# Splitting the stationary side of three float32 matmul groups into two halves of 64 columns

## The chip, the core and the metric

The kernel runs on one core of one Trainium2 chip. The metric is device time in microseconds (us) of one execution, the median of several. TensorE (PE) does the matrix products: the stationary operand is loaded into its array by a weight load (PEld in the profile), then the rows of the moving operand stream through it (PE). ScalarE (ACT), VectorE (DVE) and GpSimd (POOL) do the element-wise work, SyncE (SP) issues the transfers.

## The reference, cut to what matters

```python
X = np.fft.rfft(x, axis=1)                      # x: (8, 3136, 256)
Yr = Xr @ w_r - Xi @ w_i + b_r                  # complex 256 x 256 mix
Yi = Xr @ w_i + Xi @ w_r + b_i
Yr = np.sign(Yr) * np.maximum(np.abs(Yr) - 0.01, 0)   # Yi likewise
x = np.fft.irfft(Yr + 1j * Yi, n=3136, axis=1)
h = x.transpose(0, 2, 1) @ U @ V                # U: (3136, 32), V: (32, 3136)
u = x + h.transpose(0, 2, 1)
out = u + np.maximum(u @ w_ch1, 0) @ w_ch2      # 256 -> 1024 -> 256
```

## The kernel before

The transform of 3136 points is done as 49 times 64. For each of the 8 batches there are these stages, named by the letter that is in the names of their PSUM tiles:

- A (`psa`): the transform over 49 points, 98 partitions at a time.
- B (`psb`, function `b_mm`, and `b_early` for the first three of batch 0): the transform over 64 points with its twiddle factors. One unit takes two frequencies `k` and two halves `h` of the 256 channels, so four products: the stationary side is a 128x128 piece of the tile `t` (of `t0t` in batch 0), the moving side 128 columns of `fb`. A frequency-0 unit has a stationary side of only 64 rows (64x128).
- the mix (`psq`, `pst`), the shrinking, and C (`psc`), the inverse over 64 points.
- D (`psd`, function `d_unit`): the inverse over 49 points. One unit has four products: the stationary side is 98x128 of the tile `zt`, the moving side 130 columns of `dt` (`du` in batch 0): 98 of the transform and 32 that carry U.
- U (`psu`, function `make_ud`): once, 32 small products that make those 32 columns, 98x98 stationary by 32 moving.
- then, in windows of 512 tokens: V (`psv`), the first layer (`psy`, `psx`, `psz`; seven products in place of eight, in the manner of Strassen) and the second layer (`pso`).

There are two kinds of products. Most operands are split into a high and a low part of type float32r, and each product is done as three matmuls of the parts (`mm3`, `l1`, `l2_chunks`). B, D, U and the A stage of the first two batches multiply plain float32 in one instruction of the program, which the hardware profile shows as two passes, each with a weight load and a matmul of its own. So B and D have 384 + 512 = 896 instructions of 128 stationary columns, which are 1792 passes, and U has 32, which are 64 passes; the 64-row units of B (16 more instructions) are apart from these.

The order of all instructions is not written by hand. Every operation is first recorded with a cost (`_Program.cost`); then `order` and `forward` arrange the operations of each engine by list scheduling from these costs, and `trace` issues them, so that nearly everything in the profile has one line, L509 (L512 in the changed kernel). Operations on one PSUM tile that were recorded in a row stay together as a unit. For the PE the planner knows float32 matmuls as `port` operations; after them it charges `SWITCH` us once, and `STICK` makes it prefer to stay with them:

```python
free[e] = t + sum(op.cost for op in units[k])
if e == "pe":
    free[e] += SWITCH * (whole and not u.port)
```

In the built program 928 float32 instructions of B, D and U with full width stand in 146 unbroken groups on the PE (95 of them of 4 instructions, 25 of 8, 13 of 12, 10 of 16). Beside them five short visits of the 64-row units of B run in a 64x128 part of the array, and a few float32r matmuls of C, of the mix and of `pst` with a 64-column stationary side in its left 128x64 part.

Of the kernel before, what the change touches and what calls it, by code (L numbers as in the profile page):

```python
# [26 lines left out]
NP = 98  # L27
NI = 32
D = 256
R = 32  # L30
# [113 lines left out]


PASSES, LEAD, FILL = 12, 16.0, 200.0
SWITCH, STICK = 0.083, 5.0


CHANGES = ()  # L150
# [6 lines left out]
class _Program:  # L157
# [27 lines left out]
    def cost(self, op, out, ins):  # L185
        n = out.ids.size // out.shape[0] if isinstance(out, _View) else 1
        sb = not any(v.buf.space == "psum" for v in ins)
        op.move, op.port, op.fill = 0.0, False, 0
        if op.name == "dma_start":

            some = out if isinstance(out, _View) else ins[0]
            op.move = some.ids.size / 64000
            op.cost = 0.35 if op.eng == "act" else 0.5
            op.lag = 2.2 + op.move
        elif op.eng == "pe":
            if op.name == "matmul" and op.kw["lhsT"].dtype == F32:
                op.cost = 2 * max(0.111, 0.00084 * n)
                op.port = True
            else:
                op.cost = max(0.1118, 0.000422 * n)  # L200
            op.lag = 0.25
        elif op.eng == "act":
            op.cost = 0.17 + 0.000836 * n + (0.035 if sb else 0) + (0.09 if "bias" in op.kw else 0)
            op.lag = 0.1
        elif op.eng == "dve":

            op.port = sb and op.name != "transpose"
            slow = op.name == "transpose" and not sb
            op.cost = 0.155 + (0.00053 if op.name == "tensor_scalar" else 0.00168 if slow else 0.00104) * n
            op.lag = 0.1  # L210
        elif op.eng == "pool":
            op.port = op.name == "tensor_tensor"
            op.cost = 0.16 + (0.00222 if op.port else 0.0007) * n
            op.lag = 0.15
# [298 lines left out]
def fft_mix_moe_kernel(  # L513
# [21 lines left out]
    act, dve, pool, pe, dma = [prog.engine(e) for e in ("act", "dve", "pool", "pe", "sp")]  # L535
# [6 lines left out]
    def psm(shape, name):  # L542

        turn_m[0] += 1
        return ps_m.tile(shape, F32, tag=f"psm{turn_m[0] % 3}", name=name)
# [8 lines left out]
    def acopy(o, i):  # L554
        return act.activation(o, i, AF.Copy)
# [164 lines left out]
    def pairs(b):  # L720
        p = [(1 + 2 * q, 2) for q in range(12)]
        if shared(b):
            p.append((0, 2))
        elif b == 0 or b % 2 == 1:
            p.append((0, 1))
        return p
# [12 lines left out]
    def load_t(b, q):  # L739
        k0, n = pairs(b)[q]  # L740
        if b == 0:
            if (b, "fb", q) not in s_state:
                load_fb(b, q)
            ts = [[t0[h][:, k0 + k] for h in range(2)] for k in range(n)]
            s_state[b, q] = (ts, s_state.pop((b, "fb", q)))
            return
        t = fp.tile([128, 2, D], F32, tag="t", name=f"t_{b}_{q}")
        g = gd[b % 2]
        nk = n if k0 else 1
        dma.dma_start(t[0:64, 0:nk, :], g[k0 : k0 + nk].rearrange("k n d -> n k d"))  # L750
        if n > nk:
            dma.dma_start(t[0:64, 1, :], gd[(b + 1) % 2][0])
        if k0:
            dma.dma_start(t[64:128, 0:n, :], g[24 + k0 : 24 + k0 + n].rearrange("k n d -> n k d"))
        if (b, "fb", q) not in s_state:
            load_fb(b, q)
        ts = [[t[:, k, 128 * h : 128 * h + 128] for h in range(2)] for k in range(n)]
        s_state[b, q] = (ts, s_state.pop((b, "fb", q)))

    def ybuf(b, q, tag):  # L760

        tg = tag if b else dict(rl="xsh", ys="xsl")[tag]
        return fp.tile([128, 2, D], F32, tag=tg, name=f"{tag}_{b}_{q}", bufs=1)

    def b_early(q):

        load_t(0, q)
        ts, fbt = s_state[0, q]
        ps = psm([128, 2, 2, 128], f"psb_0_{q}")
        for k in range(2):  # L770
            pe.matmul(ps[:, 0, k, :], lhsT=ts[k][0], rhs=fbt[:, k, :], start=True, stop=True)
        s_state[0, "ps", q] = ps

    def b_mm(b, q):
        k0, n = pairs(b)[q]
        ts, fbt = s_state.pop((b, q))
        kk = 128 if k0 else 64
        early = s_state.pop((b, "ps", q), None)
        if early is not None:
            ps = early  # L780
        elif b:
            ps = ps_f.tile([128, 2, 2, 128], F32, tag="psf", name=f"psb_{b}_{q}")
        else:
            ps = psm([128, 2, 2, 128], f"psb_{b}_{q}")
        for h in range(2) if early is None else (1,):
            for k in range(n):
                pe.matmul(
                    ps[:, h, k, :],
                    lhsT=ts[k][h][:kk],
                    rhs=fbt[:kk, k if k0 else 0, :],  # L790
                    start=True,
                    stop=True,
                )
        return ps


# [230 lines left out]
    def d_load(b, t, du):  # L1027
        z_load(b, 2 * t)
        z_load(b, 2 * t + 1)
        if du is None:  # L1030
            dt_ = mp.tile([NP, TI, NP + R], F32, tag="dt", name=f"dt_{b}_{t}", bufs=2)
            i = slice(TI * t, TI * t + TI)
            dma.dma_start(dt_, dud[:, i, :])
        else:
            dt_ = du[t]
        return dt_

    def d_unit(b, i, du):
        i *= 2
        t, k = divmod(i, TI)  # L1040
        ahead = 1 if b else 3
        if i == 0:
            for c in range(ahead):
                s_state[b, "d", c] = d_load(b, c, du)
            p_state[b] = qp.tile([128, 2, R], F32, tag="pa", name=f"pa_{b}", bufs=2)
        if k == 0 and t + ahead < NT:
            s_state[b, "d", t + ahead] = d_load(b, t + ahead, du)
        if i % NH == 0:
            xq[b, i // NH] = qp.tile([128, 2, NH, NP], F32, tag="xq", name=f"xq_{b}_{i}", bufs=3)
        zt, dt_ = s_state[b, "z", i // 2], s_state[b, "d", t]  # L1050
        if b or i // 2 % 2:
            ps = ps_f.tile([128, 512], F32, tag="psf", name=f"psd_{b}_{i}")
        else:
            ps = psm([128, 512], f"psd_{b}_{i}")
        psv = ps[:, 0 : 2 * (2 * NP + R)].rearrange("p (h c) -> p h c", h=2)
        for h in range(2):
            for n in range(2):
                pe.matmul(
                    psv[:, h, n * NP : n * NP + NP + R],
                    lhsT=zt[:, n, 128 * h : 128 * h + 128],  # L1060
                    rhs=dt_[:, k + n, :],
                    start=h == 0 and n == 0,
                    stop=h == 1 and n == 1,
                    skip_group_check=True,
                )
        for h in range(2):
            c = h * (2 * NP + R)
            both = ps[:, c : c + 2 * (NP + R)].rearrange("p (n c) -> p n c", n=2)
            acopy(xq[b, i // NH][:, h, i % NH : i % NH + 2, :], both[:, :, 0:NP])
        pa = p_state[b]  # L1070
        if i == 0:
            dve.tensor_copy(pa, psv[:, :, NP : NP + R])
        else:
            dve.tensor_tensor(out=pa, in0=pa, in1=psv[:, :, NP : NP + R], op=ALU.add)
# [114 lines left out]
    for a in range(4):  # L1189
        v = (b_r, b_i)[a % 2]  # L1190
# [28 lines left out]
    us = mp.tile([NP, NI, R], F32, tag="rl", name="us", bufs=3)  # L1219
# [17 lines left out]
    fdt = qp.tile([NP, NI, NP], F32, tag="xq", name="fdt", bufs=3)  # L1237
# [10 lines left out]
    def make_ud(c):  # L1248
        ps = psm([128, 512], f"psu_{c}")
        for k in range(8):  # L1250
            pe.matmul(
                ps[:NP, 32 * k : 32 * k + 32],
                lhsT=fdt[:, 8 * c + k, :],
                rhs=us[:, 8 * c + k, :],
                start=True,
                stop=True,
            )
        for t in range(2):
            o = ps[:NP, 128 * t : 128 * t + 128]
            u = du[2 * c + t].rearrange("p (g i) c -> p g (i c)", i=2)  # L1260
            acopy(u[:, :, NP : NP + 2 * R], o.rearrange("p (g r) -> p g r", r=2 * R))
# [122 lines left out]
    def wait_2():  # L1384

        for c in range(4):
            make_ud(c)
            a_mm(1, c)
        for u in range(4, NI // 2):
            a_mm(1, u)  # L1390
# [308 lines left out]
    for w, prev, next_w in zip(turn_w, [None] + turn_w, turn_w[1:] + [None]):  # L1699
        b, j = divmod(w, NW)  # L1700
        if j == 0 and b < NB:
            assert not side
            side = [(6.5, lambda b=b: rest_unit(b))]
            if b + 1 < NB:
                start, mid, end = (1, 58, 84) if b else (18, 71, 86)

                side += bmc_spread(b + 1, start, mid - 6)
                if b + 2 < NB:
                    if shared(b + 1):
                        lo, hi = (21, 56) if b == 0 else (1, 39)  # L1710
                    else:
                        lo, hi = 45, 94
# [6 lines left out]
        for g in range(2):  # L1719
            l1s = l1_chunks(w, g)  # L1720
            new = l2_chunks(w, g)
            for k in range(4):
                for c in range(2):
                    n = WS * j + 8 * g + 2 * k + c
# [115 lines left out]
```

## Time and profile before

| | |
|---|---|
| median of 3 runs | 1624.22 us (1622.07 to 1627.01) |
| profiled execution | 1623.88 us, span in the profile 1622.1 us |
| PE busy | 1594.0 us (98%), 11112 matmul passes |
| weight loads busy | 1475.7 us (91%) |
| DVE, ACT, POOL busy | 73%, 62%, 35% |

The span is the time from the first to the last instruction of the program; it is 1.8 us shorter than the execution's own time. A matmul's record reaches from its start to the modelled end of its results, so that a record is longer than the step to the next matmul: the step of a group is (its length minus one record) divided by (its count minus 1).

### The profile page before, as it was taken

What the parts mean: (1) busy time and instruction counts of PE and PEld (TensorE: products, weight loads), DVE (VectorE), ACT (ScalarE), POOL (GpSimd) and SP (SyncE); (2) the same over time, 40 slices, a digit from 0 to 9 for tenths busy, and PEclk for the clock granted to TensorE, in tenths of its full rate; (3) what the DMA queues carried; (4) which work ended last, traced back from release to release, by engine and by line L of the source; (5) the groups of instructions that cost most, each with busy time, mean ns of one, the idle gap of its engine ahead of it and who ended that gap; (6) DMA issues with size and microseconds to landing.
All of it is one profiled execution on the core that took longest, in us unless ns stands there. A gap on an engine that the chain in (4) does not pass through costs nothing. (4 is left out here: it accounts for less than half of the span.)

```text
span 1622.1 us, 31847 instructions
## 1 busy us (share of the span) xinstructions
PE 1594.0 (98%) x11112; PEld 1475.7 (91%) x11112; DVE 1186.9 (73%) x2097; ACT 1005.1 (62%) x2187; POOL 566.5 (35%) x502
## 2 busy tenths in 40 slices
PE   8999999999999999999999999999999999999998
PEld 6979999998899999999889998999898999999997
DVE  6888777587856688577875777767785677857775
ACT  4875775565666676556666676556666666655553
POOL 2322552233433553124443554223343333312221
PEclk9999999999999999999999999999999999999999
DMA  8874555334663565414674466623557244620222
GB/s 250 237 245 116 161 170 141 114 102 131 178 200 121 146 184 140 142 53 111 170 204 137 132 174 163 166 62 92 144 148 219 83 114 132 161 77 16 54 72 53
DMA packets 271452, 223.63 MB, mean 138 GB/s; under 512 B 136986, under 2 KB 220608, under 8 KB 271292
## 3 DMA queue, kind: packets, MB, share of 16 engines
q1 hardware_dynamic: 268654, 220.73, 48.1%
q8 instruction: 89, 1.46, 0.4%
q10 hardware_dynamic: 2638, 0.86, 0.2%
q14 instruction: 71, 0.58, 0.1%
HBM read 121.36 MB, written 77.20 MB: 122 GB/s over the span
## 5 line engine op out<-in xcount | busy, mean ns | idle before, releaser
L509 PE MATMUL pso<-rh,w2t 128*128 128x512 f32 x1568 | 407.5, 382 | 0.6 <-DVE xq L509 0.6
L509 PEld LDWEIGHTS pso<-rh,w2t 128*128 128x128 f32 x1568 | 274.6, 190 | 27.6 <-DVE xq L509 1.0
L509 PE MATMUL pso<-rl,w2t 128*128 128x512 f32 x784 | 233.5, 379 | 0.5 <-DVE rl L509 0.5
L509 POOL TENSOR_TENSOR yl<-ys,yh 128x512 fp32r<-128x512 f32 (+1 forms) x101 | 132.0, 1307 | 211.0 <-ACT yh L509 190.6
L509 POOL TENSOR_TENSOR xl<-xt,xh 98x512 fp32r<-98x512 f32 x96 | 129.3, 1347 | 196.9 <-ACT xh L509 192.8
L509 DVE SCALAR_TENSOR_TENSOR rl<-s,rh 128x512 fp32r<-128x512 f32 x196 | 162.2, 839 | 11.5 <-ACT rh L509 10.7
L509 PEld LDWEIGHTS pso<-rl,w2t 128*128 128x128 f32 x784 | 148.0, 189 | 22.0 <-DVE rl L509 1.1
L509 ACT ACTIVATE rh<-s 128x512 fp32r<-128x512 f32 x196 | 121.7, 629 | 47.9 <-DVE s L509 46.3
L509 POOL TENSOR_TENSOR tl<-ts,th 128x256 fp32r<-128x256 f32 x88 | 70.3, 799 | 164.0 <-issue 70.1
L509 DVE TENSOR_TENSOR tb<-psq,bias 128x512 f32<-128x512 f32 x88 | 60.8, 691 | 88.6 <-DMA ys<-tb 48.9
L509 PE MATMUL psy<-odh,w1t 128*128 128x256 f32 x784 | 122.0, 278 | 3.3 <-DVE s L509 2.8
L509 PE MATMUL psq<-wmt,xsh 128*128 128x256 f32 (+1 forms) x704 | 122.6, 275 | 0.0
L509 PEld LDWEIGHTS psy<-odh,w1t 128*128 128x128 f32 x784 | 110.5, 191 | 11.8 <-DVE s L509 4.5
L509 ACT ACTIVATE yh<-ys 128x512 fp32r<-128x512 f32 (+1 forms) x101 | 63.4, 627 | 85.1 <-DMA ys<-tb 80.3
L509 PEld LDWEIGHTS psq<-wmt,xsh 128*128 128x128 f32 (+1 forms) x704 | 110.9, 191 | 3.0
L509 POOL TENSOR_TENSOR oal<-tt,oah 128x512 fp32r<-128x512 f32 x48 | 65.4, 1363 | 135.6 <-ACT oah L509 130.2
L509 PE MATMUL psd<-dt,zt 98*128 98x130 f32 x896 | 109.4, 275 | 2.7 <-DMA zt<-zd 1.9
L509 DVE TENSOR_TENSOR v<-v,psy 128x512 f32<-128x512 f32 x98 | 67.0, 683 | 60.5 <-ACT v L509 58.4
L509 PEld LDWEIGHTS psd<-dt,zt 98*128 98x128 f32 x896 | 105.9, 191 | 5.4 <-issue 2.7
L509 ACT ACTIVATE xq<-psd 128x196 f32<-128x196 f32 x256 | 72.0, 332 | 59.7 <-PE psd L509 59.3
L509 POOL TENSOR_TENSOR odl<-tt,odh 128x512 fp32r<-128x512 f32 x48 | 64.0, 1334 | 109.8 <-ACT odh L509 98.2
L509 PE MATMUL psq<-wmt,xsl 128*128 128x256 f32 (+1 forms) x352 | 97.2, 276 | 1.0 <-DVE xsl L509 0.9
(215 smaller groups left out, 4146.9 us busy)
## 6 DMA issues: line engine op xcount, KB each, us to landing
zt<-zd SPq DMA_DIRECT2D x128, 196.0 KB
zd<-zs SPq DMA_DIRECT2D x192, 128.0 KB
out_dram<-os SPq DMA_DIRECT2D x190, 128.0 KB
ys<-tb SPq DMA_DIRECT2D x350, 64.0 KB
t<-gd SPq DMA_DIRECT2D x168, 128.0 KB
xt<-in_x_dram SPq DMA_DIRECT2D x100, 196.0 KB
gd<-gs SPq DMA_DIRECT2D x96, 196.0 KB
fb<-in_fb_dram SPq DMA_DIRECT2D x96, 128.0 KB
```

Of the source, the lines that this page charges most:

```text
L509: call(*[real(a) for a in op.args], **{k: real(a) for k, a in op.kw.items()})
```

## The change

Each B, D and U product is written as two matmuls over 64 stationary columns each (64 and 34 for U). The moving side is the same for both. The first writes PSUM partitions 0 to 63, the second 64 to 127, so the first is built for the left 128x64 part of the array (position 0, 0) and the second for the right part (position 0, 64). The 64-row units of B stay whole. The planner's cost of such a half is 0.065 us where the whole was 0.222, and SWITCH is 0.35 in place of 0.083.

```diff
-SWITCH, STICK = 0.083, 5.0
+SWITCH, STICK = 0.35, 5.0
...
             if op.name == "matmul" and op.kw["lhsT"].dtype == F32:
-                op.cost = 2 * max(0.111, 0.00084 * n)
+                if op.kw["lhsT"].shape[1] <= 64:
+                    op.cost = max(0.065, 0.00042 * n)
+                else:
+                    op.cost = 2 * max(0.111, 0.00084 * n)
...
+    def b_half(o, t, f, cut=True):
+        for c in range(2) if cut else ():
+            v = slice(64 * c, 64 * c + 64)
+            pe.matmul(o[v], lhsT=t[:, v], rhs=f, start=True, stop=True)
+        if not cut:
+            pe.matmul(o, lhsT=t, rhs=f, start=True, stop=True)
...
-            pe.matmul(ps[:, 0, k, :], lhsT=ts[k][0], rhs=fbt[:, k, :], start=True, stop=True)
+            b_half(ps[:, 0, k, :], ts[k][0], fbt[:, k, :])
...
+                b_half(ps[:, h, k, :], ts[k][h][:kk], fbt[:kk, k if k0 else 0, :], k0 > 0)
...
-                pe.matmul(
-                    psv[:, h, n * NP : n * NP + NP + R],
-                    lhsT=zt[:, n, 128 * h : 128 * h + 128],
...
+                for c in range(2):
+                    pe.matmul(
+                        psv[64 * c : 64 * c + 64, h, n * NP : n * NP + NP + R],
+                        lhsT=zt[:, n, 128 * h + 64 * c : 128 * h + 64 * c + 64],
...
+            for lo, hi in ((0, 64), (64, NP)):
+                pe.matmul(
+                    ps[lo:hi, 32 * k : 32 * k + 32],
+                    lhsT=fdt[:, 8 * c + k, lo:hi],
...
```

In the changed program 1856 halves stand in 159 groups (103 of 8 halves, 31 of 16, 19 of 24, the rest other sizes): as many groups as before and some more, and the part of the array that an instruction is built for changes 339 times along the PE's order where it changed 24 times. The counts of transfers (1607 by SP), of ACT operations (2186) and of DVE and POOL operations are the same.

The PE's order at one B unit, the fourth of batch 4, before (names are tile, then its numbers; 128x128 is partitions written by columns moved):

```order
L509 MATMUL pst_2_9600<-wm0h,th_2_9564 128x256
L509 MATMUL pst_2_9600<-wm0l,th_2_9564 128x256
L509 MATMUL pst_2_9600<-wm0h,tl_2_9585 128x256
L509 MATMUL psb_3_9611<-fb_3_9394,t_3_9382 128x128 x4
L509 MATMUL psy_1_9408<-odh_9256,w1t 128x256 x4
L509 MATMUL psy_1_9408<-odl_9264,w1t 128x256 x2
L509 MATMUL pso_0_9481<-rh_0_1_9343,w2t 128x512
```

The four products stand alone between the mix and the first layer. Now the same unit on the PE:

```order
L512 MATMUL pso_0_10018<-rh_0_1_9866,w2t 128x512
L512 MATMUL pso_1_10021<-rh_0_1_9866,w2t 128x512
L512 MATMUL pso_0_10018<-rl_0_1_9888,w2t 128x512
L512 MATMUL pso_1_10021<-rl_0_1_9888,w2t 128x512
L512 MATMUL psb_3_10121<-fb_3_9928,t_3_9883 64x128 x8
L512 MATMUL psy_1_9913<-odh_9759,w1t 128x256 x4
L512 MATMUL psy_1_9913<-odl_9771,w1t 128x256 x2
```

Four matmuls became eight halves, which stand after a piece of the second layer; they are still a group by themselves.

The first D units of batch 4 on the PE, before (the first number of `psd` is the row pair `i`):

```order
L509 MATMUL pso_0_10899<-rl_1_0_10983,w2t 128x512
L509 MATMUL pso_1_10901<-rl_1_0_10983,w2t 128x512
L509 MATMUL psd_0_11061<-dt_0_10590,zt_0_10996 128x130 x4
L509 MATMUL psd_2_11071<-dt_0_10590,zt_1_11002 128x130 x4
L509 MATMUL psd_4_11084<-dt_1_10599,zt_2_11011 128x130 x4
L509 MATMUL psd_6_11098<-dt_1_10599,zt_3_11019 128x130 x4
L509 MATMUL psy_1_10868<-odh_10786,w1t 128x256 x4
L509 MATMUL psy_1_10868<-odl_10815,w1t 128x256 x2
L509 MATMUL psa_6_11121<-xh_6_11004,fah 98x512
```

and in the changed program:

```order
L512 MATMUL pso_0_11454<-rl_0_1_11405,w2t 128x512
L512 MATMUL pso_1_11456<-rl_0_1_11405,w2t 128x512
L512 MATMUL psd_0_11566<-dt_0_10752,zt_0_11507 64x130 x8
L512 MATMUL psd_2_11576<-dt_0_10752,zt_1_11516 64x130 x8
L512 MATMUL psy_1_11421<-odh_11277,w1t 128x256 x4
L512 MATMUL psy_1_11421<-odl_11294,w1t 128x256 x2
L512 MATMUL psd_4_11605<-dt_1_10766,zt_2_11526 64x130 x8
L512 MATMUL pso_0_11454<-rh_0_1_11392,w2t 128x512
L512 MATMUL pso_1_11456<-rh_0_1_11392,w2t 128x512
```

A group of four D units became a group of two and a group of one with a piece of the first layer between them: the larger SWITCH did not make the groups fewer here.

More of the change, by code (lines that the diff above doesn't have):

```diff
@@ L786, in b_mm @@
             for k in range(n):
-                pe.matmul(
[L788 to L793, printed above, removed]
+                b_half(ps[:, h, k, :], ts[k][h][:kk], fbt[:kk, k if k0 else 0, :], k0 > 0)
         return ps
@@ L1057, in d_unit @@
             for n in range(2):
-                pe.matmul(
-                    psv[:, h, n * NP : n * NP + NP + R],
-                    lhsT=zt[:, n, 128 * h : 128 * h + 128],
[L1061 to L1065, printed above, removed]
+                for c in range(2):
+                    pe.matmul(
+                        psv[64 * c : 64 * c + 64, h, n * NP : n * NP + NP + R],
+                        lhsT=zt[:, n, 128 * h + 64 * c : 128 * h + 64 * c + 64],
+                        rhs=dt_[:, k + n, :],
+                        start=h == 0 and n == 0,
+                        stop=h == 1 and n == 1,
+                        skip_group_check=True,
+                    )
         for h in range(2):
@@ L1250, in make_ud @@
         for k in range(8):
[L1251 to L1257, printed above, removed]
+            for lo, hi in ((0, 64), (64, NP)):
+                pe.matmul(
+                    ps[lo:hi, 32 * k : 32 * k + 32],
+                    lhsT=fdt[:, 8 * c + k, lo:hi],
+                    rhs=us[:, 8 * c + k, :],
+                    start=True,
+                    stop=True,
+                )
         for t in range(2):
```

## The prediction

> **What bounds the kernel now.** I read the page's busy times first, then the windows by stage, then the groups of the PE by form, and last the timeline around single groups, because the change touches only PE work and the price of a PE group is in its steps.
>
> ```profile
> span 1622.1 us, 31847 instructions
> PE 1594.0 (98%) x11112; PEld 1475.7 (91%) x11112; DVE 1186.9 (73%) x2097; ACT 1005.1 (62%) x2187; POOL 566.5 (35%) x502
> PEclk9999999999999999999999999999999999999999
> 300.00:1480.00 1180.00, 1168.49 (x8212) 1091.27 (x8211) 859.14 (x1543) 742.07 (x1634) 435.91 (x378) 1.00 0.48 135
> ```
>
> The reader sees a PE that is busy in 98% of the span, at the full clock; in the long middle part (the last row is a window: length, then busy time of PE, PEld, DVE, ACT, POOL) only 11.5 us of 1180 are not covered. No other engine comes above 73%. So time that the PE gains or loses in this part is gained or lost by the kernel nearly one to one, and what hides the PE's work is nothing.
>
> ```profile
> L509 PE MATMUL psd<-dt,zt 98*128 98x130 f32 x896 | 109.4, 275 | 2.7 <-DMA zt<-zd 1.9 <-DMA dt<-dud 0.7
> L509 PE MATMUL psb<-fb,t 128*128 128x128 f32 x672 | 88.7, 275 | 0.0
> L509 PE MATMUL psd<-du,zt 98*128 98x130 f32 x128 | 15.3, 276 | 0.7 <-DMA zt<-zd 0.7
> L509 PE MATMUL psb<-fb,t0t 128*128 128x128 f32 x96 | 12.7, 277 | 1.7 <-DMA fb<-in_fb_dram 0.9 <-DVE t0t L509 0.7
> 706.22 1.07 PEld L509 LDWEIGHTS psb<-fb,t 128*128 128x128 f32 x8
> 706.43 1.05 PE L509 MATMUL psb<-fb,t 128*128 128x128 f32 x8
> 282.15 2.87 PE L509 MATMUL psd<-dt,zt 98*128 98x130 f32 x24
> ```
>
> The four groups that the change rewrites hold 226.1 us of PE time (109.4 + 88.7 + 15.3 + 12.7), 14% of the span. In the timeline rows a B unit of 4 instructions is 8 passes in 1.05 us: the step is (1.05 - 0.275) / 7 = 0.1107 us. D: (2.87 - 0.275) / 23 = 0.1128. One instruction, two passes, costs 0.2214 in B and 0.2256 in D.
>
> **What sets that step** decides the case: the load of 128 columns, or the stream of 128 or 130 rows? Three more rows answer it.
>
> ```profile
> L509 PE MATMUL psa<-xx,fa 98*128 98x512 f32 x32 | 14.3, 595 | 1.1 <-DMA xx<-in_x_dram 1.1
> 89.58 1.02 PE L509 MATMUL psa<-xa,fas 98*98 98x512 f32 x2
> L509 PE MATMUL psu<-us,fdt 98*98 98x32 f32 x64 | 5.9, 249 | 0.1
> 78.52 1.49 PE L509 MATMUL psu<-us,fdt 98*98 98x32 f32 x16
> ```
>
> Two float32 passes of 512 rows take 1.02 us with a record of 0.595: the step is 0.425, so a row costs 0.00083 us and 128 rows 0.106. U streams only 32 rows (0.027) and still steps by (1.49 - 0.249) / 15 = 0.083: that is the load of 98 columns. On a line through 98 columns (0.083) and 128 (0.111) a load of 64 costs about 0.051, an estimate. So B and D are held by both at once, the load at about 0.111 and the stream at 0.106 to 0.108. Halving the columns takes away the first bound and leaves the second. Rows of the kernel with a 64-column stationary side, though float32r, show just this:
>
> ```profile
> 1390.58 0.39 PE L509 MATMUL psy<-odl,w1t 128*128 128x256 f32 x2
> 1390.80 0.38 PE L509 MATMUL psq<-wmt,xsh 128*64 128x256 f32 x2
> ...
> 1392.00 0.27 PE L509 MATMUL psq<-wmt,xsl 128*64 128x256 f32 x1
> 1392.11 0.60 PE L509 MATMUL pso<-rh,w2t 128*128 128x512 f32 x2
> ```
>
> Twelve passes begin at 1390.80 and the last at 1392.00: 0.109 per pass, with a stream as long as B's (256 rows of one cycle). The narrower load saved 0.002. I take 0.109 as the price of one half pass.
>
> **The change, part by part.**
>
> Halves. 896 instructions of B and D become 1792 halves, 3584 half passes. A half has two passes on the same part of the array, which must stream one after the other: left high, left low, right high, right low. If the parts stream side by side and matmuls start in order, the right half's first pass starts with the left half's second, and the next instruction's left half with the right half's second. In the steady state an instruction then costs two steps, 2 x 0.109 = 0.218. Saved: 384 x (0.2214 - 0.218) = 1.3 us in B and 512 x (0.2256 - 0.218) = 3.9 us in D, 5.2 together. No row shows two parts of the array at work at once. The ends are 0.436 per instruction (four steps, no overlap; the row of 0.109) and 0.111 (the stream at half its time as well, with loads side by side). I take 0.218, since the rows give the stream and say nothing against the overlap.
>
> Loads. Four loads of 64 columns, even one behind another, are 4 x 0.051 = 0.204, below 0.218: hidden behind the stream, with little room.
>
> The end of a group. The last right half begins one step after the last left half, and full-width work can't stream until it has left: one pass of 0.107 per group that today isn't there. 159 groups: 17.0 us. Lower end 0 (the order of passes could be other than I think), upper end 0.2 per group.
>
> Changing parts of the array. The nearest rows differ. The 64-column visit above costs nothing on either side: the second `psy` starts at 1390.69, `psq` 0.11 later, and `pso` 0.11 after the last `psq`. The 64-row visit of B costs much:
>
> ```profile
> 249.32 0.39 PE L509 MATMUL psy<-odl,w1t 128*128 128x256 f32 x2
> 249.63 0.96 PEld L509 LDWEIGHTS psb<-fb,t 64*128 64x128 f32 x8
> 249.63 1.16 PE L509 MATMUL psb<-fb,t 64*128 64x128 f32 x8
> 250.72 0.71 PE L509 MATMUL psz<-obh,w1t 128*128 128x256 f32 x4
> ...
> 709.96 0.61 PE L509 MATMUL psz<-obh,w1t 128*128 128x256 f32 x4
> ```
>
> The second `psy` starts at 249.43, the load of `psb` only at 249.63, and eight passes take 1.16 in place of 1.05: the PE runs dry and the first load is exposed, 0.20 - 0.11 + 0.11 = 0.20. At the end the last `psb` starts at 250.515 (249.63 + 1.16 - 0.275), `psz` at 250.72, and its four passes take 0.71, where four such passes elsewhere take 0.61 (the last row): again 0.19. Ends: 0 and 0.39 per group, 0 and 62 us over 159 groups. I take 0, because the 64-column visit is the nearer row: same shape of the part, only the right half is new. The Trainium skill ("TensorEngine Tiling (Array Packing)", Key Properties) says that changing the tiling mode drains the engine. By that rule the sum would be 62 us higher; the 64-row rows here agree with it at 0.2 per side, the 64-column rows do not show it.
>
> U. 64 passes of 0.083 become 64 of 64 columns and 64 of 34, whose loads sum to the same columns. Ends: half of it gone (-2.7 us) and all of it twice (+5.3); taken as 0.
>
> The order. The planner now thinks B and D cheaper and changing dearer, and all engines' rows move; no transfer, ACT, DVE or POOL operation is added. What idles today on the PE is 1622.1 - 1594.0 = 28 us in all, most of it at the start and the end. A new order can lose or win some of it; I take 0, with 8 us either way. Evictions of `psb` and `psd` come 0.1 us later at most, beside ACT at 62% and DVE at 73%.
>
> **Sum.** -5.2 + 17.0 + 0 + 0 + 0 = +11.8 us. The profiled execution has 1623.9 us, 0.3 us below the median of the three runs, so this becomes about 1636 us.
>
> **Rivals.**
>
> 1. Changing parts drains the PE, as at the 64-row visits. For it: 0.39 us per visit in the rows above, and the right half at a new place. Against it: the 64-column rows. Place: both ends of each of 159 groups. 11.8 + 62 = +74: 1698 us.
>
> 2. The halves do not run side by side, so the change does not do what it says. For it: a pass of 64 columns costs 0.109, as much as one of 128, and no two matmuls of this trace overlap in their streams. Against it: nothing in the trace tries two parts. Then 896 x (0.436 - 0.2235) = +190 us: 1814 us. Here 0.2235 is the mean of 0.2214 and 0.2256.
>
> 3. The other side: faster. A float32 pass costs 0.00083 us per row where float32r costs half of that (`psq`: 256 rows in 0.109). If a 64-column part takes its rows at the float32r rate, a half pass streams in 0.055, and with both parts side by side, loads too, an instruction costs 0.111: 896 x (0.2235 - 0.111) = 101 us saved, against a tail of 159 x 0.056 = 9: -92 us, 1532 us. With the full price of changing, 62 us, -30: 1594 us. It decides for faster as soon as an instruction of B or D costs under 0.20 with free changes, or under about 0.13 with dear ones. Against it: the step at 512 rows is the stream's own, and nothing shows that it depends on the columns. For it: that rate is the only thing that keeps the step at 0.107 once the load is halved, and the trace has no float32 pass of 64 columns that would rule it out.
>
> The Trainium skill has a rule for the overlap ("TensorE: Matmul & The Clock Gate", Packing small matmuls): matmuls on different parts of the array run at the same time, yet start and end strictly in program order. No run here shows it. With it the sum stays at +11.8; a start out of order would take the 17 us of tails away.
>
> **How the numbers follow.** A time within 0.3% (4.9 us) counts as no change, about what a measurement of this kernel can tell. Overlap with free changes, my forecast: 0.33, of which 0.19 slower (tails as priced), 0.12 within 0.3% (tails smaller, or a better order) and 0.02 faster. Rival 1: 0.23. Rival 2: 0.14. Rival 3: 0.30, most of it (0.22) with changes that cost something. So faster 0.32, same 0.12, slower 0.56. The forecast's own range is 1611 (no tails, a better order) to 1648. Cases of both signs are open, so the range reaches from rival 3 with dear changes less the 8 us of the order, 1585, to rival 1 with 7 us of it, 1705; it leaves out rival 2 and rival 3 with free changes, 0.22 in all.
>
> **What would show it.** Right: the group of 8 halves of a B unit (16 half passes) spans about 0.98 us from its first start to the next full-width one (4 x 0.218 + 0.107), against 0.89 today; a load record of 64 columns near 0.136 us, as at `psq`. The first full-width load after a group tells of rival 1: directly behind the last half, or 0.2 us and more after it. Rival 2 would show 1.74 us for the same group and PE busy near 1780; rival 3 under 0.6 before the change of parts. What would make the forecast wrong: a float32 pass whose rate depends on its columns, or loads of the right part that wait for the left part's stream.

## The result, and the profile after

The changed kernel takes 1675.87 us (median of 4, 1674.24 to 1679.29), the kernel before 1624.21 us: a ratio of 1.032, 95% interval 1.0296 to 1.0343, 52 us slower. The forecast had the sign, with 1636 us, and less than a quarter of the size (11.8 of 52 us). The profiled execution took 1674.24 us, 50.4 us more than the one of before. All times in this document are of executions at a granted clock of 0.99 or more; one of the first experiment, 2699.37 us at 0.653, is left out.

The page's head and the window of the middle stage of the changed kernel (length, then busy time of PE, PEld, DVE, ACT, POOL):

```profile
span 1672.5 us, 35597 instructions
PE 1645.3 (98%) x12992; PEld 1474.7 (88%) x12992; DVE 1176.8 (70%) x2097; ACT 1010.3 (60%) x2187; POOL 566.1 (34%) x502
300.00:1530.00 1230.00, 1219.17 (x9726) 1101.71 (x9723) 851.98 (x1554) 750.82 (x1655) 437.75 (x380) 1.00 0.47 132
```

The PE is as full as before, 98%, at the full clock, and the other engines have the same work in a longer span: the 50 us are the PE's own. The gaps shown below do not lower the 98%, since a matmul's record reaches on to the end of its results and so covers them. The groups of B and D by form:

```profile
L512 PE MATMUL psd<-dt,zt 98*64 98x130 f32 x1792 | 111.7, 277 | 0.2 <-DMA zt<-zd 0.2
L512 PE MATMUL psb<-fb,t 128*64 128x128 f32 x1344 | 92.8, 281 | 4.1 <-DVE tb L512 2.1 <-DVE xq L512 1.9
L512 PE MATMUL psd<-du,zt 98*64 98x130 f32 x256 | 15.8, 276 | 0.0
L512 PE MATMUL psb<-fb,t0t 128*64 128x128 f32 x192 | 13.1, 278 | 0.8 <-DVE t0t L512 0.8
```

Twice as many passes keep the PE busy for 233.4 us (111.7 + 92.8 + 15.8 + 13.1) where it was 226.1. So the halves do run side by side: one behind another they would take about twice as long. The loss is not inside the groups but at their ends. A B unit and a group of three D units in the timeline:

```profile
768.98 0.59 PE L512 MATMUL pso<-rl,w2t 128*128 128x512 f32 x2
769.50 0.85 PEld L512 LDWEIGHTS psb<-fb,t 128*64 128x64 f32 x16 [0.33 <-issue]
769.50 1.09 PE L512 MATMUL psb<-fb,t 128*64 128x128 f32 x16
770.52 0.52 PEld L512 LDWEIGHTS psy<-oah,w1t 128*128 128x128 f32 x4 [0.17 <-issue]
...
1077.55 2.65 PEld L512 LDWEIGHTS psd<-dt,zt 98*64 98x64 f32 x48 [0.33 <-issue]
1077.55 2.90 PE L512 MATMUL psd<-dt,zt 98*64 98x130 f32 x48
1080.38 0.52 PEld L512 LDWEIGHTS psy<-obh,w1t 128*128 128x128 f32 x4 [0.17 <-issue]
```

What to see. The second `pso` starts at 769.19 (768.98 + 0.59 - 0.379) and its 512 rows are through at 769.405. The first load of `psb` begins only at 769.50, and its 64 columns, 0.05 us, are exposed: the PE streams nothing for 0.15 us. The last `psb` starts at 770.32 (769.50 + 1.09 - 0.272) and is through at about 770.425; the load of `psy` begins at 770.52 and its 128 columns, 0.107 us, are exposed: 0.20 us more. "issue" in the brackets means that the load waited for nothing that the profile shows. In between 16 half passes stream in 0.87 us, 0.0544 each or 0.218 per instruction of the kernel before, 0.223 when D's 48 are counted the same way. Three D units pay the same two gaps as one B unit.

Put together from all matmul records (the distance between the ends of neighbouring records, less the usual step of the form: 0.216 for 512 rows, 0.112 for 256 and for a whole float32 pass, 0.055 for a half pass), before against after: the steps in and around the groups of B, D and U hold 8.4 us of excess with wholes (5.9 of it at D) and 62.8 with halves, +54.4 or 0.34 for each of 159 groups; the excess of all other steps goes from 24.7 to 23.4, -1.3; the narrower loads give 896 x (0.2238 - 0.220) = -3.4. The sum is +49.7, for 50.4 in the spans.

### The profile page after: what moved, and what is told of

Read it like the earlier page. It is cut to its first block, busy times and chain, and to the rows that moved or that the text cites. A ratio compares the mean times of both kernels' runs of the same rounds, so it can differ in the third digit from the quotient of the medians.

```text
span 1672.5 us, 35597 instructions
## 1 busy us (share of the span) xinstructions
PE 1645.3 (98%) x12992; PEld 1474.7 (88%) x12992; DVE 1176.8 (70%) x2097; ACT 1010.3 (60%) x2187; POOL 566.1 (34%) x502
## 4 chain that ended last, share of the span: by engine, by line
PE 86%; DVE 4%; SPq 4%; DMA 3%; issue 2%; ACT 0%; POOL 0%; DVEq 0%; ACTq 0%; POOLq 0%
PE pso L512 28%; PE psy L512 17%; PE psd L512 7%; PE psx L512 7%; PE psq L512 6%; PE psb L512 5%; PE psa L512 5%; SPq L512 4%; PE psz L512 4%; PE psc L512 3%; PE pst L512 3%; DMA ys<-tb 2%; DVE tb L512 1%; PE psv L512 1%; DMA xt<-in_x_dram 0%
## 5 line engine op out<-in xcount | busy, mean ns | idle before, releaser
L512 DVE SCALAR_TENSOR_TENSOR rl<-s,rh 128x512 fp32r<-128x512 f32 x196 | 156.7, 809 | 17.7 <-ACT rh L512 17.0
L512 PE MATMUL psd<-dt,zt 98*64 98x130 f32 x1792 | 111.7, 277 | 0.2 <-DMA zt<-zd 0.2
L512 PEld LDWEIGHTS psd<-dt,zt 98*64 98x64 f32 x1792 | 98.5, 136 | 12.6 <-issue 8.6
L512 PE MATMUL psb<-fb,t 128*64 128x128 f32 (+1 forms) x1372 | 97.0, 281 | 4.1 <-DVE tb L512 2.1
```

Of the source, the lines that this page charges most:

```text
L512: call(*[real(a) for a in op.args], **{k: real(a) for k, a in op.kw.items()})
```

## The experiments

Theory 1: every change between full-width work and float32 halves costs about 0.35 us per group, whatever the group's size, and the halves themselves are as good as whole. Theory 2: the loss is the planner's new order. Theory 3: the loss goes with the halves themselves.

**The changed order without the halves.** Halves are planned, wholes are issued:

```diff
+            if op.emit == "skip":            # the first half of a pair
+                continue
+            if op.emit is not None:          # the second: out, lhsT and rhs of the whole
+                op.args, op.kw = op.emit
             call = getattr(engines[op.eng], op.name)
```

> Planned as the changed kernel is, with its costs and its halves, but each pair of halves is issued as one matmul of 128 columns: the changed order without the halves. Theory 1 (each group of halves pays about 0.35 us for changing the part of the array, 159 groups): the loss is gone, 1624 us within 8, steps of 0.111 to 0.113 in B and D, no gaps round the groups. Theory 2 (the new order, made from wrong costs, is what loses): 1660 to 1676 us, with PE waiting for other engines.

Measured: 1640.48 us (median of seven), ratio 1.0075 (1.0054 to 1.0097), 12 us. The same place in its timeline has no gaps:

```profile
751.42 0.59 PE L516 MATMUL pso<-rl,w2t 128*128 128x512 f32 x2
751.64 1.07 PEld L516 LDWEIGHTS psb<-fb,t 128*128 128x128 f32 x8
751.86 1.05 PE L516 MATMUL psb<-fb,t 128*128 128x128 f32 x8
752.64 0.53 PEld L516 LDWEIGHTS psy<-oah,w1t 128*128 128x128 f32 x4
```

Most of the loss went with the halves, yet the order alone costs 12 us: more than the 8 that theory 1 allowed, far less than theory 2 gave it. Its PE waits for other engines 28.1 us in the view of waits, against 20.5 before. The PE's order here is that of the changed kernel, so the two can be set side by side, by the same sum over the records: with halves the steps in and around the groups rise from 10.3 to 62.8 us (+52.5, 0.33 per group), all other excess steps fall from 34.3 to 23.4 (-10.9), and the narrower loads give -3.4. That is 38 us, for 36.2 between the spans. So of the 50.4 us between the spans of the kernels before and after, 14.2 are the order's (12 by the ratio of the times above) and 36.2 the halves', and the gaps cover about 11 us of waits.

**What triggers the gap: one extra half in a full-width kernel.** One left half ahead of each D unit of the kernel before, or one right half:

```diff
+        pe.matmul(psv[0:64, 0, 0 : NP + R], lhsT=zt[:, 0, 0:64], rhs=dt_[:, k, :],
+                  start=True, stop=True, skip_group_check=True)   # right: 64:128 in both
```

> The kernel before, with one float32 half of 64 columns in the left part added ahead of each D unit's first matmul, which overwrites it: 128 more instructions, 256 passes, each a group by itself among full-width work. Theory 1a (any float32 matmul of 64 columns changes the mode, whichever part it uses): per extra half 0.21 us of stream and 0.35 of change, 128 x 0.56 = 72 us, 1696 us. Theory 1b (only the right part, or going between the parts, costs): stream alone, 128 x 0.21 = 27 us, 1651 us, no gap in the trace.

> The same with the extra half in the right part. Theory 1a and theory 1b both: 0.21 + 0.35 us each, 1696 us, with gaps of 0.15 us ahead of the half and 0.2 behind it. Against theory 1 altogether: 1651 us.

Measured: 1695.38 us (ratio 1.0411, 1.0356 to 1.0466) and 1693.74 us (1.0401, 1.0339 to 1.0462), two executions each. Theory 1a holds in both: the left part pays as the right does. The timeline of the left one, then two rows of the right one:

```profile
709.10 0.19 PEld L509 LDWEIGHTS psd<-dt,zt 98*64 98x64 f32 x2 [0.33 <-issue]
709.46 1.28 PEld L509 LDWEIGHTS psd<-dt,zt 98*128 98x128 f32 x10 [0.17 <-issue]
...
705.41 0.19 PEld L509 LDWEIGHTS psd<-dt,zt 98*64 98x64 f32 x2 [0.33 <-issue]
705.77 1.28 PEld L509 LDWEIGHTS psd<-dt,zt 98*128 98x128 f32 x10 [0.17 <-issue]
```

The load's idle time ahead of the half is the same 0.33 as in the changed kernel, the one behind it the same 0.17, though what follows the half is a whole matmul of the same unit with the same operands. And in the changed kernel itself the float32r matmuls with 64 columns still have none (the second `pso` starts at 1439.57, `psq` 0.22 later, the length of that stream):

```profile
1439.35 0.59 PE L512 MATMUL pso<-rl,w2t 128*128 128x512 f32 x2
1439.57 0.35 PEld L512 LDWEIGHTS psq<-wmt,xsh 128*64 128x64 f32 x2
1439.79 0.38 PE L512 MATMUL psq<-wmt,xsh 128*64 128x256 f32 x2
```

So neither 64 columns nor the left place tells whether the PE drains (stands without a stream until the next load is in): with the same shape and place, float32 drained and float32r did not. One place goes further: in the run with the planner's measured price (below) a float32r visit of 64 columns stands directly behind U's halves.

```profile
93.25 1.12 PE L513 MATMUL psu<-us,fdt 98*64 98x32 f32 x32
94.30 0.13 PEld L513 LDWEIGHTS psc<-yh,fc0h 128*64 128x64 f32 x1
94.59 0.28 PE L513 MATMUL psc<-yl,fc0h 128*64 128x256 f32 x1
94.70 1.02 PE L513 MATMUL psa<-xa,fas 98*98 98x512 f32 x2
```

The last half of U starts at 94.15 (93.25 + 1.12 - 0.223), and its 32 rows are through after 0.027 us. The load of `psc` begins only at 94.30, so the stream stops although neither side is of full width. Behind the visit full-width `psa` follows with no gap, 0.11 us after the last `psc`. There the float32r visit behaved as full-width work does. It is a single place, where a wait for an operand is not excluded either; why the number type decides is not shown.

**All left halves of a D unit first, then all right ones**, and **two and two**:

```diff
-        for h in range(2):
-            for n in range(2):
-                for c in range(2):
+        for c in range(2):              # two and two: for h, for c, for n
+            for h in range(2):
+                for n in range(2):
```

> The changed kernel, but a D unit issues its four left halves first and then its four right halves. If the two parts have queues of their own, which may run ahead of the program's order (as the pairs that start 7 ns apart suggest): D still steps by about 0.055 us per half pass, 1676 us within 8. If matmuls start in the program's order (as the prediction supposed): no overlap but at the seam, a D unit takes 15 steps of 0.109 in place of 8, 128 x 0.76 = 97 us more, 1773 us.

> The changed kernel, but a D unit issues two left halves, two right, two left, two right. If the right part may start while about three passes of the left one are still to come (as in the run with all four left halves first, where the right part began when three left passes were open): the parts run one or two passes apart, 0.1 to 0.2 us more per group of D, 62 groups, 6 to 12 us: 1682 to 1688 us. If matmuls had to start in program order: 1720 us or more.

Measured: 1716.25 us (ratio 1.0542, 1.0497 to 1.0587) and 1679.23 us (1.0338, 1.0323 to 1.0354). The first lies between its two expectations, 40 us above the changed kernel; the second 3 us above it, a little better than expected. These 3 us lie within the intervals of the two times, but D's rows bear them out: its PE time is 131.2 us (115.0 + 16.2) in place of 127.5 (111.7 + 15.8). One D unit, left halves first, then two and two:

```profile
705.37 1.36 PEld L512 LDWEIGHTS psd<-dt,zt 98*64 98x64 f32 x16
705.37 1.61 PE L512 MATMUL psd<-dt,zt 98*64 98x130 f32 x16
...
690.13 1.16 PE L512 MATMUL psd<-dt,zt 98*64 98x130 f32 x16
```

One part alone needs 8 x 0.109 = 0.87 for its eight passes. From the first start to the last it took 1.34 us (1.61 - 0.275) with the lefts first, 0.89 two and two, 0.84 in the changed kernel, where 0.76 (7 x 0.109) is the least. In the records of the first, the left part's passes run from the start at steps of 0.11, and the right part's begin 0.50 us in, when five left passes have started and three are still to come. So a part may start ahead of earlier matmuls of the other part, here when three of their passes were left; strictly in order it could not start before the last of them.

**D alone and B alone, each planned anew.** Only one of the two is cut, the planner's new numbers stay:

```diff
     def b_half(o, t, f, cut=True):
+        cut = False          # D alone; for B alone d_unit's loop is undone instead
```

> Only D in halves, B and U whole; 62 groups of halves. Theory 1: 62 x 0.35 = 22 us for the changes, less 512 x 0.0064 = 3 us for the narrower loads: +19 us, 1643 us. If the loss goes by halves and not by groups (theory 3): 1024 of 1856 halves, 55% of 52 us, 1653 us.

> Only B in halves, D and U whole; 94 groups of halves. Theory 1: 94 x 0.35 = 33 us, less 384 x 0.0022 = 1 us: +32 us, 1656 us. Theory 3 (by halves): 768 of 1856, 41% of 52 us, 1645 us.

Measured: 1671.14 us (1.028, 1.0257 to 1.0304) and 1643.85 us (1.0107, 1.0089 to 1.0125). Neither theory had it: D with 62 groups loses 45 us, B with 94 loses 17. The two differ in order as well as in halves: the PE waits for other engines 37.3 us in the one and 12.1 in the other. By the same sum over the records D's own steps rose by 17 us and all others by 31; B's own rose by 32, and all others fell by 10. A time in which the order moves along decides nothing here; so the next three keep it.

**Halves in the old order.** Planned as the kernel before; only the issue cuts each whole matmul of the named stages in two:

```diff
+            if op.kw["lhsT"].shape[1] > 64 and str(op.out.buf.kw["name"])[:3] in ("psb", "psd", "psu"):
+                for v in (slice(0, 64), slice(64, op.kw["lhsT"].shape[1])):
+                    kw = dict(op.kw, lhsT=op.kw["lhsT"][:, v])
+                    call(real(op.args[0][v]), **{k: real(a) for k, a in kw.items()})
+                continue
```

> All halves, but planned with the costs of the kernel before, so in its order: each matmul of B, D and U of full width is issued as a left and a right half where it stood. 146 groups. Theory 1: the gap at both ends of a group, 0.35 us, in the place of nothing: 146 x 0.35 = 51 us, less 896 x 0.0045 = 4 us, less up to 10 us because a gap also covers waits that the PE has anyway: 1661 to 1671 us. If most of the loss was the planner's new order: under 1645 us.

> As before this one, with D alone in halves: 50 groups in the old order. Theory 1: 50 x 0.35 = 17 us, less 512 x 0.0064 = 3 us: 1638 us (1632 to 1640). The same half of the change under the planner's new costs took 1671 us: if D itself is dear, it is again above 1660 us.

> B alone in halves in the old order: 93 groups. Theory 1: 93 x 0.35 = 33 us, less 384 x 0.0022 = 1 us, less up to 8 us of waits that the gaps cover: 1648 to 1656 us.

Measured: all 1659.47 us (1.0219, 1.0202 to 1.0235), D 1642.07 (1.0119, 1.0101 to 1.0137), B 1642.04 (1.0113, 1.0098 to 1.0128). Now the parts add up: 18.2 + 18.2 us against 35.6 for both. With all halves the B unit looks as in the changed kernel:

```profile
762.28 0.39 PE L515 MATMUL psx<-ocl,w1t 128*128 128x256 f32 x2
762.60 0.85 PEld L513 LDWEIGHTS psb<-fb,t 128*64 128x64 f32 x16
763.62 0.73 PEld L515 LDWEIGHTS pso<-rh,w2t 128*128 128x128 f32 x4 [0.17 <-issue]
```

B came out 6 us under its expectation, all halves 2 us under, D 2 us above. The same sum over the records tells why. The PE's order is that of the kernel before, so each cell compares the same steps, before and then with halves:

| halves in the old order | groups | in and around the named groups | other excess steps | narrower loads | sum | spans |
|---|---|---|---|---|---|---|
| all | 146 | 8.4 to 57.2: +48.8 | 24.7 to 16.5: -8.2 | -3.4 | +37.2 | +35.3 |
| D | 50 | 5.9 to 23.6: +17.7 | 27.2 to 29.0: +1.8 | -2.3 | +17.2 | +17.3 |
| B | 93 | 1.9 to 35.0: +33.1 | 31.2 to 17.6: -13.6 | -1.3 | +18.2 | +18.2 |

A group costs 0.33 to 0.36 us in all three, B's as much as D's. With D alone nothing of it comes back elsewhere; with B alone 14 us do. Work that waited for another engine in the kernel before finds its operand ready, since the PE comes later: the view of waits falls from 20.5 to 14.0 us, which names about half of these 14. Why this happens behind B's groups and not behind D's was not found out.

**The planner with the measured price** (a half at 0.1095 us):

```diff
-                    op.cost = max(0.065, 0.00042 * n)
+                    op.cost = 0.1095
```

> The changed kernel with one number of the planner mended: a half of B or D costs 0.1095 us (measured: two half passes of 0.0548) in place of 0.065; SWITCH stays 0.35. 148 groups of halves where there were 159. If the rest of the loss beyond the halves in the old order (1659 us) came from planning with halves that are too cheap: 1655 to 1664 us. If any new order loses as much: 1672 to 1680 us.

Measured: 1670.66 us, ratio 1.0266 (1.0244 to 1.0288), between the two expectations and nearer to the second. By the ratios the right price saves about 9 us of the 52; planned anew, the kernel still loses about 8 us against the halves in the old order, with 25.5 us of waits where that one has 15.4. Which of the moved operations cause these waits was not found out.

**Taking away the changes that the kernel already had.** The five 64-row visits of B are made full-width, on rows of zeros:

```diff
-        kk = 128 if k0 else 64
+        kk = 128
...
+        if not k0:
+            pool.memset(t[64:128, 0:n, :], 0.0)
```

> The kernel before with full-width float32 matmuls, and its five 64-row visits of B made 128 rows deep as well (the lower 64 rows of the tile hold zeros), so that no float32 matmul leaves the full array. Theory 1: 5 x 0.39 = 2 us less, 1622 us, no gap at these visits. If the gap there is not the change of the part: the same time as before, gaps still there.

Measured: 1625.66 us (median of 12), ratio 0.9997 (0.9985 to 1.0009). The visits now run at full width, and their 1.9 us of gaps are gone from the records, but the planner's order moved with the memsets, and the excess of all other steps, those of B, D and U among them, rose from 33.1 to 40.9 us in the profiled execution. No version here beats the kernel before by more than can be measured.

## Why the prediction was right or wrong

- **What bounds the kernel**: right. The PE was the bound in every run, and its gaps came through, except where they covered waits that were there anyway; that exception was not in the prediction and is worth 11 us in the changed kernel's order and 8 in the old one.
- **The step of a half**: right. 0.218 us per instruction was forecast; 0.218 was found in B and 0.223 in D, and the saving was 3.4 us where 5.2 were forecast. The overlap, which no row showed, is there. This settles rivals 2 (0.436) and 3 (0.111): a float32 half pass streams as long as a whole one.
- **The end of a group**, +17.0 us: wrong. The two parts do not start left, left, right, right; the first starts of a group lie 0.007 us apart, and so do the last ones. The term measured 159 x 0.007 = 1 us. The page of the Trainium skill that was quoted for the start in program order ("TensorE: Matmul & The Clock Gate", Packing small matmuls) is not borne out by the run with the left halves first.
- **Changing parts of the array**, taken as 0: this is the step that failed. It measured 0.35 us at a lone B unit, 0.15 ahead of it and 0.20 behind, and +54 us over 159 groups, 0.34 each. The choice of the nearest row was the error: the 64-column visits agreed in shape and place, the 64-row visits in number type, and it was the second that held. The price then stood in the rows: 0.39 per visit. The drain that the Trainium skill states ("TensorEngine Tiling (Array Packing)", Key Properties) is there for float32; the 64-column float32r visits show none beside full-width work in any run.
- **U**, taken as 0: about 0, from two sizes that cancel. It is the one group whose step the load alone set, and there halving shortened it: a pair of half passes, 64 and 34 columns, steps by (1.12 - 0.224) / 31 x 2 = 0.058 us (1.12 us for 32 half passes, in the row of U further above) where the whole pass took 0.083. Over 64 passes that is 1.6 us less, against 1.4 for the gaps of its four groups, an estimate (4 x 0.35).
- **The order**, 0 with 8 us either way: too small. The order alone costs 12 us, and D alone planned anew lost 45 where the same halves in the old order lost 18.
- **Rival 1**, 1698 us, is the mechanism that came true. It was 22 us too high: 17 of it is the tail that does not exist, the rest is smaller gaps (0.35 for 0.39) and covered waits, with the order's loss against them.

## What to carry to other kernels

A full 128-column float32 matmul that moves 128 rows has almost nothing to gain from being cut into two column halves: the halves overlap, but together they stream as long as the whole, and every visit stops the PE's stream twice, here 0.35 us. Only where the load sets the step, as with U's 32 rows, did the cut shorten it. What it gains where columns would otherwise be empty was not tried here. Keep such work in long groups, since the price is per visit. When a price is taken from the nearest row, compare the number type as well as the shape; and when a planner's costs change along with the code, test the code in the old order first, or the order's own gain or loss is read as the code's.

## What the runs showed of the hardware

- Left and right float32 halves run as two streams that are not held to the program's order: passes start 0.007 us apart, and with four left halves ahead of four right ones the right part started when three earlier passes of the left were still to come. Grain matters: against alternating halves, two and two cost 3 us, four and four 40 us.
- Going between full-width work and 64-column float32 work leaves the PE without a stream for 0.15 us on the way in and 0.20 on the way out; the exposed weight load is 0.05 and 0.107 of it. 64-column float32r work in the left part leaves none beside full-width work.
- Weight loads of the two parts overlap too: U's pair of 64 and 34 columns steps by 0.058 us where the load of 98 columns in one piece stepped by 0.083.
- A gap on the bounding engine does not add up blindly: in the old order 49 us of gaps lengthened the span by 35, as other excess steps of the same engine shrank by 8 and the narrower loads took 3 off; the last 2 are not placed.
